# Moving columns of the feed-forward products taken in turn from two places

## The chip, the cores and the metric

The kernel runs on one core of a Trainium2 chip. The metric is the device time of one execution in microseconds. Three executions of the kernel before took 502.5, 500.82 and 500.69 us; their median is 500.82 us. One further execution was profiled. It took 500.46 us, of which 498.7 us lie between its first and its last recorded instruction; that stretch is called the span below, and times inside it are counted from its start.

## The reference, cut to what matters

A gated linear attention over 4 batches, 8 heads, 768 steps and head size 48 gives the rows of a feed-forward part with 384 inputs, 2048 hidden units and 384 outputs.

```python
def _attn_ref(q, k, v, f_logit):
    f = 1.0 / (1.0 + np.exp(-f_logit))
    for t in range(S):
        state = f[:, :, t, :, None] * state + np.einsum('bhd,bhe->bhde', k[:, :, t], v[:, :, t])
        y[:, :, t] = np.einsum('bhd,bhde->bhe', q[:, :, t], state)

def _moe_ref(x, w_in, w_out):
    h = x @ w_in
    relu6 = np.clip(h + 3.0, 0.0, 6.0)
    g = h * relu6 / 6.0
    return (g @ w_out).astype(np.float32)
```

Here x has 3072 rows: 4 batches times 768 steps.

## The kernel before, in words

**Tiling.** The 768 steps are cut into 6 chunks of 128. A unit is one batch and one chunk, so there are 24 units. The attention of a unit ends in rows of x, transposed (features on partitions, steps along the free dimension). The four units of one chunk, one for each batch, make a group with 4 x 128 = 512 columns. The feed-forward part (FF) runs group by group, and in a group over 16 blocks of 128 hidden units, called f.

**Two halves of every number.** A float32 value is held as a high part and a low part, each in the type float32r, which the multiplier array takes in one pass. A product of two values is then three products: high by high, high by low, low by high (the table `P3`). The tile `xts` holds x: for each of 3 blocks of features and each batch 128 high columns and after them 128 low columns, so the high columns of the four batches stand 1 KB apart. The tile `weight` holds both halves of both weight matrices.

**One f of one group.** `mm1` makes 3 x 3 = 9 products of 512 columns into one PSUM bank (L561; the banks are called `pair` and `single`). ScalarE makes the clipped value `tg` out of it (`relu`, L571), VectorE multiplies by h (`gate6`, L575), ScalarE takes the high half `gg` (`ghigh`, L584) and VectorE the low half (`glow`, L588). `mm2` makes 3 x 3 = 9 products from `gg` into three PSUM banks `o`, one for each 128 outputs (L605). In these products the weights stand still in the array, and the 512 columns of `xts` or `gg` move through it; mm1 reads them as four runs of 128, mm2 as one run of 512. After the 16th f the `o` banks are copied to `os` in SBUF, by VectorE (L669) or ScalarE (L671), and sent out by DMA (`put`, L676).

**Exceptions.** The first three f of group 0 are done in two halves of 256 columns (`half_of`, L623 for the first product, L641 for the second). Their second product takes plain float32, with no split: each is one call with 256 columns, and the array is given two instructions for a call (36 matmul instructions for 18 calls). In the last group the third block of outputs is done in two halves of 256 columns (`half_mm2`, L656), and the hidden halves are kept in `xts` in place of `gg`. A slow path for inputs that end a chunk with a very small decay is in the program and does not run with these inputs.

**Order.** All engines follow one list of steps written out by hand (`ORDER`). It fixes the order of every engine's instructions; waits come from what reads and writes what. `warm` steps in the list are products of a constant zero tile in bf16 (L777), whose 512 moving columns are one block of 128 read four times.

The functions that the change touches:

Of the kernel before, what the change touches and what calls it, by code (L numbers as in the profile page):

```python
# [8 lines left out]
F32 = mybir.dt.float32  # L9
# [10 lines left out]
C = 128  # L20
HC = C // 2
# [136 lines left out]
def gla_moe(ctx: ExitStack, tc: tile.TileContext, unit, w, outT):  # L158
# [16 lines left out]
    def bank():  # L175

        n = banks.pop(0) if banks else 0
        return single if n == 4 else pairs[n // 2][:, n % 2]
# [8 lines left out]
    def whole(f, a, cols):  # L187
        return weight[:, f, a * WN:(a + 1) * WN][:, cols]

    def win(f, a, k):  # L190
        return whole(f, a, slice(k * 128, (k + 1) * 128))

    def wout(f, a, m):
        return whole(f, a, slice(DM + m * 128, DM + (m + 1) * 128))
# [356 lines left out]
    def rows_of(g):  # L551
        if "xt" not in g:
            g["xt"] = xts[:, KT:][:, ::-1] if g["odd"] else xts[:, :KT + 1]
        return g["xt"]

    def mm1(g, f):
        h = bank()[:, :g["n"]]
        i = 0
        for a, b in P3:
            for k in range(KT):  # L560
                nc.tensor.matmul(  # L561
                    h, win(f, a, k), g["xt"][:, k, :g["n"] // C, b],
                    start=i == 0, stop=i == 3 * KT - 1,
                )
                i += 1
        g[f] = {"h": h}
# [25 lines left out]
    def outs_of(g, f):  # L592
        if f == 0:
            g["o"] = [
                ps_o.tile([128, 512], F32, tag=f"o{x}", name=f"o{g['name']}_{x}")[:, :g["n"]]
                for x in range(KT)
            ]

    def mm2(g, f, ms=range(KT)):
        if 0 in ms:  # L600
            outs_of(g, f)
        for i in range(3):
            a, b = P3[-i]
            for m in ms:
                nc.tensor.matmul(  # L605
                    g["o"][m], wout(f, a, m), g[f]["gg"][:, b],
                    start=f == 0 and i == 0, stop=f == NF - 1 and i == 2, skip_group_check=True,
                )

    def mm2_whole(g, f):  # L610
        outs_of(g, f)
        for m in range(KT):
            nc.tensor.matmul(
                g["o"][m], wout(f, 1, m).bitcast(F32), g[f]["t"],
                start=f == 0, stop=f == NF - 1, skip_group_check=True,
            )

    def half_of(p):

        def mm1(g, f):  # L620
            h = bank()[:, :256]
            for i, (a, b, k) in enumerate((a, b, k) for a, b in P3 for k in range(KT)):
                nc.tensor.matmul(  # L623
                    h, win(f, a, k), g["xt"][:, k, 2 * p:2 * p + 2, b],
                    start=i == 0, stop=i == 3 * KT - 1,
                )
            g[f, p] = {"h": h}

        def relu(g, f):
            d = g[f, p]  # L630
            d["t"] = sb.tile([128, 512], F32, tag="tg", name=f"th{p}_{f}")[:, :256]
            nc.scalar.activation(d["t"], d["h"], AF.Relu, bias=half, scale=1.0 / 6.0)

        def gate6(g, f):
            d = g[f, p]
            nc.vector.scalar_tensor_tensor(d["t"], d["t"], 1.0, d["h"], op0=ALU.min, op1=ALU.mult)

        def mm2(g, f):
            outs_of(g, f + p)
            for m in range(KT):  # L640
                nc.tensor.matmul(  # L641
                    g["o"][m][:, p * 256:(p + 1) * 256],
                    wout(f, 1, m).bitcast(F32), g[f, p]["t"],
                    start=f + p == 0, stop=False, skip_group_check=True,
                )

        return {"mm1": mm1, "relu": relu, "g": gate6, "mm2": mm2}

    def half_mm2(g, f, part):

        n = g["n"] // 2
        if f == 0:
            g["oh", part] = bank()[:, :n]
        for i in range(3):
            a, b = P3[-i]
            nc.tensor.matmul(  # L656
                g["oh", part], wout(f, a, 2), g[f]["gg"][:, b, part * n:(part + 1) * n],
                start=f == 0 and i == 0, stop=f == NF - 1 and i == 2, skip_group_check=True,
            )

    def out(g, m, part, on_vector):
        n = g["n"] if part is None else g["n"] // 2
        if "os" not in g:
            held = cv.tile([128, 4 * WN + 4], I16, tag="raw", name=f"os{g['name']}")
            g["os"] = held[:, :4 * WN].bitcast(F32).rearrange("p (m n) -> p m n", m=KT)
        os = g["os"][:, m, n * (part or 0):n * (part or 0) + n]
        src = g["o"][m] if part is None else g["oh", part]
        if on_vector:
            nc.vector.tensor_copy(out=os, in_=src)  # L669
        else:  # L670
            nc.scalar.activation(os, src, AF.Copy)  # L671
        g["os", m, part] = os

    def put(g, m, part=None):
        n = (g["n"] if part is None else g["n"] // 2) // C
# [5 lines left out]
    def group(name, n, dst):  # L681
        return {"name": name, "n": n, "dst": dst, "odd": len(groups) % 2}
# [26 lines left out]
    def smallest_flag():  # L709
# [5 lines left out]

    MOE = {
        "mm1": mm1, "relu": relu, "g": gate6, "gh": ghigh, "gl": glow, "mm2": mm2, "mm2x": mm2_whole,
        "mm2m0": lambda g, f: mm2(g, f, [0]), "mm2m1": lambda g, f: mm2(g, f, [1]),
        "mm2p": lambda g, f: half_mm2(g, f, 0), "mm2q": lambda g, f: half_mm2(g, f, 1),
    }  # L720
    for p, part in enumerate("ab"):
        MOE.update({op + part: step for op, step in half_of(p).items()})
    OUT = {
        "outv": lambda g, m: out(g, m, None, True), "outs": lambda g, m: out(g, m, None, False),
        "outh": lambda g, p: out(g, 2, p, p == 0), "od": put, "odh": lambda g, p: put(g, 2, p),
    }
    FLAG = {"flag0": smallest_rows, "flag1": smallest_turn, "flag2": smallest_flag}
# [81 lines left out]
    with tc.If(rv > 0):  # L809
        with tc.For_i(0, B, 1) as b:  # L810
            st = sb.tile([PR, NP, 128], F32, tag="qkf", name="st_s")
            nc.vector.memset(st, 0.0)
            with tc.For_i(0, NCB, 1) as c:
                u = b * NCB + c
                t = sb.tile([PR, 2, NP, C], F32, tag="qkf", name="t_s")
                ft = sb.tile([PR, NP, C], F32, tag="qkf", name="f_s")
                src = qk[bass.ds(u, 1), :PR].rearrange("a p x n c -> p (a x) n c")
                nc.sync.dma_start(out=t, in_=src)
                th = t.rearrange("r x (c n) (o t) -> r x n c o t", c=2, o=2)
                src = fg[bass.ds(u, 1), :PR, 1:].rearrange("a p (n c) -> p (a n) c", n=NP)  # L820
# [3 lines left out]
                for t0 in range(0, C, TS):  # L824
# [29 lines left out]
                g = group("_s", C, lambda m: outT[m * 128:(m + 1) * 128, bass.ds((c * B + b) * C, C)].rearrange(  # L854
                    "m (b t) -> m b t", t=C
                ))
# [3 lines left out]
                for f in range(NF):  # L860
                    for step in (mm1, relu, gate6, ghigh, glow, mm2):
                        step(g, f)
                for m in range(KT):
                    out(g, m, None, m == 1)
                    put(g, m)
# [55 lines left out]
```

## Time and profile before

| quantity | value |
|---|---|
| median of three executions | 500.82 us |
| profiled execution, its own time | 500.46 us |
| span of the profiled execution | 498.7 us |
| TensorE matmul (PE) busy | 485.0 us, 97% |
| TensorE weight load (PEld) busy | 388.7 us, 78% |
| VectorE (DVE) busy | 292.6 us, 59% |
| ScalarE (ACT) busy | 217.6 us, 44% |
| GpSimd (POOL) busy | 53.7 us, 11% |
| mean granted TensorE clock | 0.992 |

In the rows of the profile, `L605 PE MATMUL o<-gg,weight 128*128 128x512 f32 x693 | 173.3, 399` would read: line 605, engine, operation, output tile and input tiles, 128 rows by 128 columns of weights, 128 partitions by 512 moving columns, 693 instructions; then the time during which at least one of them ran, and the mean length of one in ns. Products overlap: the next starts while the last is still on its way through the array. The length of one therefore says little, and the distance from start to start is what a product costs in a row of them.

### The profile page before, as it was taken

The page shows a single profiled execution, that of the slowest core. Times are in us where ns is not written, and L with a number is a line of the kernel's source. Part 1 is how long each engine was busy: PE and PEld are TensorE (multiplying, and loading weights), DVE is VectorE, ACT ScalarE, POOL GpSimd, SP SyncE. Part 2 cuts the span into 40 slices and gives each one's busy share as a digit, 9 for nine tenths or more (in the row PEclk, how much of TensorE's full clock was granted, in tenths as well). Part 3 has the DMA queues.
Part 4 walks back from the last instruction along what each step waited for, and adds up shares of the span by engine and source line. Part 5 has one row for each costly group of instructions (what it writes and reads, how often), then busy time and mean ns, then how long its engine had stood idle before and what let it go on. Part 6 is the DMA issues. An engine that isn't in the chain of part 4 may idle for free.

```text
span 498.7 us, 11481 instructions
## 1 busy us (share of the span) xinstructions
PE 485.0 (97%) x4958; PEld 388.7 (78%) x4958; DVE 292.6 (59%) x462; ACT 217.6 (44%) x372; POOL 53.7 (11%) x57
## 2 busy tenths in 40 slices
PE   8798999999999999999999999999999999999996
PEld 4587787777888888788888888887877888788885
DVE  6969999989684636757405576545642243333341
ACT  5778988754343315433305434224422232333331
POOL 2311521203200110211000010100100000000000
PEclk9979999999999999999999999999999999999999
DMA  8776765442320330523100133300300000100001
GB/s 298 269 256 238 233 207 202 132 140 82 106 83 1 114 97 1 192 75 123 52 0 3 60 130 95 105 8 2 105 24 6 24 2 0 64 0 1 0 1 69
DMA packets 18969, 44.91 MB, mean 90 GB/s; under 512 B 2528, under 2 KB 8544, under 8 KB 18912
## 3 DMA queue, kind: packets, MB, share of 16 engines
q1 hardware_dynamic: 18768, 43.98, 26.7%
q8 instruction: 41, 0.67, 0.6%
q10 hardware_dynamic: 144, 0.13, 0.1%
q14 instruction: 16, 0.13, 0.1%
HBM read 36.43 MB, written 4.72 MB: 83 GB/s over the span
## 4 chain that ended last, share of the span: by engine, by line
PE 86%; DMA 6%; DVE 4%; ACT 2%; issue 0%; POOL 0%; SPq 0%; POOLq 0%; DVEq 0%; ACTq 0%
PE o L605 35%; PE pair L561 25%; PE single L561 12%; DMA raw<-w 3%; PE pair L488 2%; PE pair L505 2%; PE pair L418 2%; PE pair L456 2%; DMA qkf<-unit 1%; PE single L656 1%; PE pair L656 1%; PE o L641 1%; PE pair L437 1%; PE pair L623 1%; DMA v<-unit 1%; DVE w L285 1%
## 5 line engine op out<-in xcount | busy, mean ns | idle before, releaser
L605 PE MATMUL o<-gg,weight 128*128 128x512 f32 x693 | 173.3, 399 | 1.2 <-DVE gg L588 1.2
L605 PEld LDWEIGHTS o<-gg,weight 128*128 128x128 f32 x693 | 128.0, 188 | 32.8 <-DVE gg L588 2.5
L561 PE MATMUL pair<-xts,weight 128*128 128x512 f32 x576 | 142.2, 396 | 0.1
L561 PEld LDWEIGHTS pair<-xts,weight 128*128 128x128 f32 x576 | 107.1, 188 | 24.9 <-DVE weight L293 0.6
L588 DVE TENSOR_TENSOR gg<-tg,gg 128x512 fp32r<-128x512 f32 x77 | 52.6, 687 | 68.4 <-ACT gg L584 68.3
L584 ACT ACTIVATE gg<-tg 128x512 fp32r<-128x512 f32 x77 | 48.2, 629 | 90.9 <-PE o L605 76.2
L575 DVE SCALAR_TENSOR_TENSOR tg<-tg,pair 128x512 f32<-128x512 f32 x64 | 42.8, 682 | 56.4 <-ACT tg L571 56.3
L571 ACT ACTIVATE tg<-pair,half 128x512 f32<-128x512 f32 x64 | 43.4, 685 | 63.0 <-PE pair L561 55.8
L561 PE MATMUL single<-xts,weight 128*128 128x512 f32 x261 | 66.5, 399 | 0.0
L561 PEld LDWEIGHTS single<-xts,weight 128*128 128x128 f32 x261 | 48.2, 188 | 11.0
L374 DVE TENSOR_TENSOR_SCAN gates<-gates,rend 112x516 f32<-112x516 f32 x24 | 33.1, 1380 | 0.2
L571 ACT ACTIVATE tg<-single,half 128x512 f32<-128x512 f32 x29 | 19.8, 683 | 28.0 <-PE single L561 24.9
L350 DVE TENSOR_TENSOR_SCAN suffix<-gates,unit 112x516 f32<-112x516 f32 x24 | 30.4, 1265 | 2.8 <-ACT gates L344 2.8
L363 POOL TENSOR_TENSOR qkf<-qkf,suffix 112x512 f32<-112x512 f32 x13 | 18.8, 1443 | 95.5 <-DVE rend L366 24.1
L379 POOL TENSOR_TENSOR qkf<-qkf,gates 112x512 f32<-112x512 f32 x13 | 17.4, 1345 | 85.1 <-DVE gates L374 40.4
L524 ACT ACTIVATE xts<-pair 112x512 fp32r<-112x512 f32 x24 | 14.3, 596 | 27.2 <-PE pair L456 13.6
L605 PE MATMUL o<-xts,weight 128*128 128x512 f32 x96 | 25.3, 397 | 0.6 <-ACT xts L584 0.6
L575 DVE SCALAR_TENSOR_TENSOR tg<-tg,single 128x512 f32<-128x512 f32 x29 | 19.7, 680 | 10.4 <-ACT tg L571 10.3
L425 DVE TENSOR_TENSOR a<-pair,causal 128x512 f32<-128x512 f32 x24 | 16.4, 682 | 10.6 <-PE pair L505 9.2
L605 PEld LDWEIGHTS o<-xts,weight 128*128 128x128 f32 x96 | 17.8, 188 | 5.4 <-ACT xts L584 1.0
L537 DVE TENSOR_TENSOR xts<-pair,xts 112x512 fp32r<-112x512 f32 x19 | 13.0, 685 | 11.4 <-ACT xts L524 11.4
L588 DVE TENSOR_TENSOR xts<-tg,xts 128x512 fp32r<-128x512 f32 x16 | 11.1, 693 | 11.3 <-ACT xts L584 11.3
(92 smaller groups left out, 449.1 us busy)
## 6 DMA issues: line engine op xcount, KB each, us to landing
qkf<-unit SPq DMA_DIRECT2D x24, 512.0 KB, 4.2
raw<-w SPq DMA_DIRECT2D x16, 768.0 KB, 5.4
gates<-unit SPq DMA_DIRECT2D x24, 258.5 KB, 2.9
v<-unit SPq DMA_DIRECT2D x24, 200.0 KB, 4.1
outT<-os SPq DMA_DIRECT2D x17, 256.0 KB, 2.1
xts<-xts SPq DMA_DIRECT2D x48, 48.0 KB, 2.2
weight<-w SPq DMA_DIRECT2D x3, 192.0 KB, 2.8
outT<-os SPq DMA_DIRECT2D x1, 128.0 KB, 3.7
```

What stands on the lines that cost most here:

```text
L350: nc.vector.tensor_tensor_scan(flat(sf)[:, ::-1], gt[:, 1:][:, ::-1], flat(unit)[:, ::-1], 0.0, op0=ALU.mult, op1=ALU.add,)
L363: engine("kmul", i).tensor_tensor(parts_of(t, 1), parts_of(t, 1), split(sf[:, :, 1:C + 1]), op=ALU.mult)
L374: nc.vector.tensor_tensor_scan(past, past, flat(rend), 0.0, op0=ALU.mult, op1=ALU.add)
L379: engine("qmul", i).tensor_tensor(parts_of(t, 0), parts_of(t, 0), split(to), op=ALU.mult)
L425: nc.vector.tensor_tensor(d["a"].rearrange("r p e t -> r e p t"), d["at"], causal.unsqueeze(1).unsqueeze(1).broadcast_to([128, 2, NP, HC]) ...
L524: nc.scalar.activation(parts(0), d["y"][:PR], AF.Copy)
L561: nc.tensor.matmul(h, win(f, a, k), g["xt"][:, k, :g["n"] // C, b], start=i == 0, stop=i == 3 * KT - 1,)
L571: nc.scalar.activation(d["t"], d["h"], AF.Relu, bias=half, scale=1.0 / 6.0)
L575: nc.vector.scalar_tensor_tensor(d["t"], d["t"], 1.0, d["h"], op0=ALU.min, op1=ALU.mult)
L584: nc.scalar.activation(d["gg"][:, 0], d["t"], AF.Copy)
L588: engine("gl", f if g["name"] == "0" else NU).tensor_tensor(d["gg"][:, 1], d["t"], d["gg"][:, 0].bitcast(F32), op=ALU.subtract)
L605: nc.tensor.matmul(g["o"][m], wout(f, a, m), g[f]["gg"][:, b], start=f == 0 and i == 0, stop=f == NF - 1 and i == 2, skip_group_check=True,)
```

## The change

Every moving operand of an FF product is read in another order. In `mm1`, instead of batch 0, then batch 1, then 2, then 3, a column of batch 0 is followed by the same step's column of batch 1, and so on for 128 steps; then the same with batches 2 and 3. In `mm2`, in each 256 columns a column of the first 128 is followed by one of the second 128. The stored tiles keep their layout; only the access patterns of the products change. Since the product writes its output columns in the order in which they come in, `h`, `tg` and `gg` now have mixed columns, and the `o` banks have them mixed twice: column 4c + q of each 256 belongs to place 64q + c. The copies to `os` undo this: they read PSUM in order and write to SBUF with a step of 64 columns (256 bytes) from one element to the next. Of the products that run, L561, L605, L623, L641 and L656 change (L614, in `mm2_whole`, is in no step of the list). The attention, the conversion of the weights, the sizes and counts of all instructions, and the order of instructions on every engine are as before (line numbers apart).

```diff
+    def turned(x):
+        if x.shape[1] == 1:
+            return x
+        return x.rearrange("p (h b) c -> p h c b", b=2)
+
+    def halves_of(x):
+        if x.shape[1] % 256:
+            return x
+        return x.rearrange("p (h b c) -> p h c b", b=2, c=128)
+
     def mm1(g, f):
...
-                    h, win(f, a, k), g["xt"][:, k, :g["n"] // C, b],
+                    h, win(f, a, k), turned(g["xt"][:, k, :g["n"] // C, b]),
...
     def mm2(g, f, ms=range(KT)):
...
-                    g["o"][m], wout(f, a, m), g[f]["gg"][:, b],
+                    g["o"][m], wout(f, a, m), halves_of(g[f]["gg"][:, b]),
...
     def mm2_whole(g, f):
...
-                g["o"][m], wout(f, 1, m).bitcast(F32), g[f]["t"],
+                g["o"][m], wout(f, 1, m).bitcast(F32), halves_of(g[f]["t"]),
...
     def half_of(p):
...
-                    h, win(f, a, k), g["xt"][:, k, 2 * p:2 * p + 2, b],
+                    h, win(f, a, k), turned(g["xt"][:, k, 2 * p:2 * p + 2, b]),
...
-                    wout(f, 1, m).bitcast(F32), g[f, p]["t"],
+                    wout(f, 1, m).bitcast(F32), halves_of(g[f, p]["t"]),
...
     def half_mm2(g, f, part):
...
-                g["oh", part], wout(f, a, 2), g[f]["gg"][:, b, part * n:(part + 1) * n],
+                g["oh", part], wout(f, a, 2), halves_of(g[f]["gg"][:, b, part * n:(part + 1) * n]),
...
     def out(g, m, part, on_vector):
...
         src = g["o"][m] if part is None else g["oh", part]
+        g["os", m, part] = os
+        if n % 256 == 0:
+            os = os.rearrange("p (h q c) -> p h c q", q=4, c=HC)
+            src = src.rearrange("p (h c q) -> p h c q", q=4, c=HC)
         if on_vector:
             nc.vector.tensor_copy(out=os, in_=src)
         else:
             nc.scalar.activation(os, src, AF.Copy)
-        g["os", m, part] = os
```

## The prediction, made before the changed kernel ran

> **What bounds the kernel now.** I read the page first: busy shares, the chain of waits, the costliest groups.
>
> ```profile
> span 498.7 us, 11481 instructions
> PE 485.0 (97%) x4958; PEld 388.7 (78%) x4958; DVE 292.6 (59%) x462; ACT 217.6 (44%) x372; POOL 53.7 (11%) x57
> PE 86%; DMA 6%; DVE 4%; ACT 2%; issue 0%; POOL 0%; SPq 0%; POOLq 0%; DVEq 0%; ACTq 0%
> L605 PE MATMUL o<-gg,weight 128*128 128x512 f32 x693 | 173.3, 399 | 1.2 <-DVE gg L588 1.2
> L561 PE MATMUL pair<-xts,weight 128*128 128x512 f32 x576 | 142.2, 396 | 0.1
> L561 PE MATMUL single<-xts,weight 128*128 128x512 f32 x261 | 66.5, 399 | 0.0
> ```
>
> TensorE is busy nearly all the time and makes up 86% of the chain that ended last, and the products that the change touches (L605, L561) are by far the largest groups in it. So what one of these products costs in a row of them sets the time. The view by stretches (time; PE, PEld, DVE, ACT, POOL busy; clock) says where this holds:
>
> ```profile
> 60.00:110.00 50.00, 48.66 (x508) 38.16 (x507) 47.66 (x75) 37.98 (x56) 10.50 (x7) 1.00 0.54 178
> 110.00:200.00 90.00, 90.00 (x1057) 72.79 (x1056) 59.58 (x94) 34.00 (x65) 11.56 (x10) 1.00 0.21 68
> 200.00:300.00 100.00, 100.00 (x1034) 80.93 (x1033) 54.89 (x87) 35.80 (x64) 10.82 (x10) 1.00 0.25 79
> 300.00:420.00 120.00, 119.82 (x1114) 96.49 (x1113) 55.47 (x87) 40.12 (x72) 5.06 (x5) 1.00 0.12 39
> 434.00:487.00 53.00, 53.00 (x263) 44.40 (x262) 18.48 (x30) 17.88 (x27) 0.00 (x0) 1.00 0.00 1
> ```
>
> From 110 us on TensorE alone is full, at full granted clock; VectorE is at two thirds or less. Before 110 us VectorE is full too (47.66 of 50 us), so a quicker product buys little there.
>
> **What a product costs.** The next rows are pieces of the chain (start, length, what, count), then one of the view by stretches for the bf16 products of L777 alone.
>
> ```profile
> 173.02 10.49 PE pair L561 x45
> 183.52 8.40 PE o L605 x36
> 491.72 1.07 PE single L656 x9
> 46.10 1.31 PE o L641 x6
> 7.72:8.80 1.08, 1.08 (x5) 0.49 (x6) 1.00 1.01 384
> ```
>
> mm1: 10.49 / 45 = 233.1 ns for 512 columns. mm2: 8.40 / 36 = 233.3 ns. The half of L656: 1.07 / 9 = 119 ns for 256 columns. A bf16 product of 512 columns took 1.08 / 5 = 216 ns, at the same clock of 1.00. Plain float32 (L641) took 1.31 / 6 = 218 ns for an instruction of 256 columns; if each column passes twice, as the length suggests, that is 218 ns for 512 passes. So the array can take a column in 0.42 ns, and float32r products lose 17 ns in 512 columns and about 10 in 256: a loss mostly by column. It is gone where a column has half the bytes (bf16) or twice the time (plain float32), so it lies in bringing in 4 bytes for every column, not in the array or the PSUM write. Where mm1 jumps 1 KB between its four runs, it costs the same as mm2's single run, so a jump now and then is free.
>
> **The change part by part.**
>
> *Reading in turn.* Two streams now give every other column. The trace has no product that jumps at every column, so I bound it. Below: each place gets twice the time for its next word, as in L641, and the whole loss goes: 233.2 − 216 = 17 ns less. Above: a read brings two neighbouring words, of which one is now used, so a product takes twice as long: 233 ns more. Between them stands ScalarE, which reads every second word in L251:
>
> ```profile
> L251 ACT ACTIVATE w<-raw 128x768 int32<-128x768 uint32 x16 | 14.5, 904 | 0.2 <-DVE weight L293 0.2
> L290 ACT ACTIVATE weight<-w 128x768 fp32r<-128x768 f32 x16 | 13.4, 840 | 5.0 <-DVE w L285 5.0
> ```
>
> It pays 904 − 840 = 64 ns for 768 words, 0.083 ns a word; at that price a product would cost 43 ns more. I take the lower end, −17 ns. [...] That is a choice, not a proof, and both other ends stay as rivals.
>
> Now the count. The view by stretches of each line alone gives the products after 110 us:
>
> ```profile
> 110.00:420.00 310.00, 139.90 (x571) 105.95 (x569) 1.00 0.19 60
> 420.00:434.00 14.00, 5.93 (x25) 4.69 (x26) 1.00 0.16 57
> 434.00:498.70 64.70, 30.15 (x121) 21.64 (x119) 0.99 0.04 14
> 110.00:420.00 310.00, 146.55 (x590) 109.45 (x591) 1.00 0.19 60
> 420.00:434.00 14.00, 7.59 (x29) 4.92 (x27) 1.00 0.16 57
> 434.00:498.70 64.70, 23.22 (x90) 16.85 (x90) 0.99 0.04 14
> ```
>
> L561 (first three rows) and L605: 571 + 25 + 121 + 590 + 29 + 90 = 1426 products. 1426 x 17 ns = 24.2 us. L656 adds 96 halves at 10 ns: 1.0 us. Before 110 us there are 1626 − 1426 = 200 more (693 + 96 + 576 + 261 in all); 200 x 17 = 3.4 us, but VectorE is full there, so I count 0.5 us. Plain float32 (L641) shows no loss and gains nothing. Together −25.7 us.
>
> *Copies that restore the order.* Eighteen in full or half (L669, L671) now write with 256 bytes between elements. Unchanged in number, reads in order. Most lie under mm1 of the next group, which writes other banks. Where they lie on the chain:
>
> ```profile
> 427.02 1.08 ACT os L671 x2
> 428.10 0.58 ACT tg L571
> 429.44 0.64 ACT xts L584
> 430.12 1.22 PE o L605 x3
> 493.89 0.38 ACT os L671
> L285 DVE SCALAR_TENSOR_TENSOR w<-top,w 128x768 int16<-128x768 int16 x16 | 16.8, 1049 | 0.5
> L575 DVE SCALAR_TENSOR_TENSOR tg<-tg,pair 128x512 f32<-128x512 f32 x64 | 42.8, 682 | 56.4 <-ACT tg L571 56.3
> L636 DVE SCALAR_TENSOR_TENSOR th<-th,pair 128x256 f32<-128x256 f32 x5 | 2.0, 418 | 1.0 <-ACT th L632 1.0
> ```
>
> At 427 us two copies on ScalarE precede the first `relu` of the last group, and TensorE waits behind them; at 494 us the last half copy ends the kernel. The nearest spaced write is L285 (2 bytes in every 4): 768 elements in 1049 ns, where the step from L636 to L575 (264 ns for 256) makes 682 + 264 = 946 for an even write: 0.13 ns an element, 70 ns a copy. Free at the one end, twice as long at the other (0.54 us each at 427, 0.38 at the end: +1.5 us). I take 0.1 us each, +0.3 us.
>
> *The wait that gets longer.* At 430 us TensorE stands idle for the chain of ScalarE and VectorE from those copies. Its own mm1 ahead of it gets 9 x 17 ns = 0.15 us shorter, so the idle time grows by that: +0.2 us. In the rest of the last group an f takes 2.10 us of mm1 and 0.70 of mm2, and the steps between them 0.69 + 0.69 + 0.63 + 0.69 = 2.7 us; mm2 runs one mm1 later than its own, so over 1 us of slack is left when an f shrinks from 2.8 to 2.6 us.
>
> **The sum.** 498.7 − 25.7 + 0.3 + 0.2 = 473.5 us of span. The profiled run had 500.46 − 498.7 = 1.8 us outside the span, and the median is 0.4 us above that run: 475.7. I forecast **476 us**, 5% faster. Half the loss removed would give 488; the full loss without any give-back 473 or a little less. The forecast's own range is 470 to 498.
>
> **The rivals.**
>
> *A. The order of reading does not matter.* If the loss is a ceiling on bytes that come in (512 columns of 4 bytes in 233 ns), two streams share it as one did. For it: mm1 and mm2, with different runs, cost 233.1 and 233.3 ns. Against it: it needs a ceiling that sits just 7% under what the array takes. Time: 500.8 + 0.3 for the copies = 501 us.
>
> *B. Every jump costs a read.* If words come in pairs and the second is thrown away, a product takes 466 ns: 1426 x 233 = 332 us, 96 x 119 ns = 11 us, and the early products, 200 x 233 + 54 x 119 ns = 53 us, nearly all to be paid, since TensorE is almost full there too (48.66 of 50): about 890 us. At ScalarE's price of 43 ns it would be 1426 x 43 ns = 61 us: about 565. For it: L251 pays something. The loss itself says that reading has no slack: two words at a time at just the pace needed would show no loss in bf16 and plain float32, and a small one here. Against it: 17 ns is far from a doubling, and where each column comes from one of only two places, a pair once read can serve twice if it is kept.
>
> [...]
>
> *C. Reading gains nothing and the spaced copies hurt.* At 427 us both copies stand ahead of a `relu` that TensorE waits for, and a group's `o` banks are freed only by its copies. It decides from about +0.9 us a copy on (2 at 427, 1 at the end, 2.7 us). At 1 us more each, and as much at the four other group ends where mm1 no longer covers them: 503.5 to 508 us.
>
> **Chances.** Forecast (loss wholly or partly gone) 0.54; A 0.21; B 0.18; C or another small loss 0.07. Measurement can tell about 0.5%, that is 2.5 us, from no change. So faster 0.54, same 0.21, slower 0.25. The range 470 to 512 holds nearly all of the forecast, A and C, together 0.8, and leaves out B, which would lie far above.
>
> **What would show it.** Right: nine products of mm1 in the chain fall from 2.10 us to about 1.95, mm2 likewise, nine halves of L656 from 1.07 to about 0.98, L641 stays at 1.31 for six, and TensorE stays full after 110 us. Pieces of 2.10 us as before mean A; of 4 us, or 2.5, mean B. Longer L669 and L671 with longer idle time before L605 at the group ends mean C. The forecast is also wrong if the products get quicker but VectorE or ScalarE chains fill the gap: then TensorE's busy share falls while the span stays.

## The result and the profile after

The changed kernel took 480.86 us (median of four executions, 476.12 to 481.75) against 500.75 us for the kernel before, measured beside it: a ratio of 0.958 with a 95% interval of 0.951 to 0.965. It is faster, as forecast, by 4.2% where 5% was forecast. Ratios are those of fast executions: one of e10_both (533.4 us, granted clock 0.844) and one of e12_second_only (493.61 us, 0.986), both below, are slow ones and stay out of them. The profiled execution took 481.13 us with a span of 479.4 us. In the changed kernel L561 has become L573, L605 L617, L641 L653, L656 L668, and the copies L669 and L671 have become L685 and L687.

The same pieces of the chain of waits as in the prediction (start, length, what, count), now of the changed kernel:

```profile
172.28 9.71 PE pair L573 x45
181.99 7.77 PE o L617 x36
471.09 1.00 PE single L668 x9
46.38 1.64 PE o L653 x6
409.93 1.98 ACT os L687 x2
411.91 0.45 ACT tg L583
413.79 0.70 PE o L617 x2
473.13 0.60 ACT os L687
```

A product of 512 columns now costs 9.71 / 45 = 215.8 ns in the first matrix and 7.77 / 36 = 215.8 ns in the second: what the bf16 product took (216 ns), with nothing left of the 17 ns. The half of L668 fell from 119 to 111 ns. Against that, plain float32 (L653) rose from 218 to 273 ns an instruction, and the copies are far slower than assumed: two on ScalarE take 1.98 us instead of 1.08, the half copy at the end 0.60 instead of 0.38.

The page's groups say the same of all copies and of the idle time before the second product (`| idle before`), which was 1.2 and 0.6 us:

```profile
L617 PE MATMUL o<-gg,weight 128*128 128x512 f32 x693 | 161.4, 383 | 2.5 <-DVE gg L600 2.4
L617 PE MATMUL o<-xts,weight 128*128 128x512 f32 x96 | 23.7, 381 | 1.6 <-ACT xts L596 1.5
L653 PE MATMUL o<-th,weight 128*128 128x256 f32 x36 | 10.8, 435 | 0.0
L687 ACT ACTIVATE os<-o 128x512 f32<-128x512 f32 x11 | 11.4, 1090 | 8.2 <-PE o L617 8.2
L685 DVE COPY os<-o 128x512 f32<-128x512 f32 x6 | 6.4, 1064 | 8.6 <-PE o L617 8.6
```

And the view by stretches (time; PE, PEld, DVE, ACT, POOL busy; granted clock), with five rows of the changed kernel and then the first product alone, up to 110 us, in the kernel before and in the changed one:

```profile
0.00:60.00 60.00, 53.27 (x793) 38.92 (x794) 46.43 (x76) 43.90 (x75) 13.69 (x25) 0.89 0.76 259
60.00:110.00 50.00, 46.74 (x598) 38.33 (x597) 47.95 (x75) 41.81 (x58) 10.50 (x6) 1.00 0.53 182
110.00:200.00 90.00, 89.65 (x1168) 77.50 (x1167) 65.04 (x104) 36.70 (x70) 13.57 (x12) 1.00 0.23 73
200.00:300.00 100.00, 100.00 (x1097) 87.14 (x1097) 59.23 (x92) 41.53 (x72) 10.21 (x10) 1.00 0.26 85
300.00:420.00 120.00, 118.15 (x1023) 102.09 (x1022) 56.59 (x88) 42.29 (x72) 5.10 (x5) 1.00 0.11 36
...
0.00:110.00 110.00, 30.78 (x124) 23.02 (x125) 0.97 0.67 224
...
0.00:110.00 110.00, 26.62 (x113) 20.85 (x114) 0.94 0.66 224
```

In the first 60 us this execution was granted 0.89 of the clock. By 110 us it had begun 113 of the first products, the kernel before 124 (the second products stand at 81 in both): the changed kernel was 11 products, some 2.4 us, behind there, and made its gain afterwards, with TensorE nearly full again.

### The profile page after: what moved, and what is told of

The parts are those of the page before. It is cut to its first block, busy times and chain, and to the rows that moved or that the text cites. A ratio compares the mean times of both kernels' runs of the same rounds, so it can differ in the third digit from the quotient of the medians.

```text
span 479.4 us, 11485 instructions
## 1 busy us (share of the span) xinstructions
PE 460.9 (96%) x4958; PEld 391.5 (82%) x4958; DVE 295.9 (62%) x462; ACT 225.4 (47%) x372; POOL 53.1 (11%) x57
## 4 chain that ended last, share of the span: by engine, by line
PE 80%; DVE 8%; DMA 4%; ACT 4%; issue 2%; SPq 0%; POOL 0%; DVEq 0%; ACTq 0%
PE o L617 32%; PE pair L573 22%; PE single L573 10%; DMA raw<-w 3%; PE pair L488 2%; PE pair L505 2%; PE o L653 2%; PE pair L418 2%; PE pair L456 2%; PE pair L635 1%; PE pair L668 1%; PE single L668 1%; DMA v<-unit 1%; DVE w L285 1%; DVE tg L587 1%
## 5 line engine op out<-in xcount | busy, mean ns | idle before, releaser
L617 PE MATMUL o<-gg,weight 128*128 128x512 f32 x693 | 161.4, 383 | 2.5 <-DVE gg L600 2.4
L617 PEld LDWEIGHTS o<-gg,weight 128*128 128x128 f32 x693 | 128.8, 189 | 22.2 <-DVE gg L600 4.1
L573 PE MATMUL pair<-xts,weight 128*128 128x512 f32 x576 | 132.7, 381 | 0.8 <-DVE weight L293 0.8
L573 PEld LDWEIGHTS pair<-xts,weight 128*128 128x128 f32 x576 | 107.5, 189 | 16.3 <-DVE weight L293 1.2
L600 DVE TENSOR_TENSOR gg<-tg,gg 128x512 fp32r<-128x512 f32 x77 | 53.8, 703 | 58.2 <-ACT gg L596 57.9
L573 PE MATMUL single<-xts,weight 128*128 128x512 f32 x261 | 62.2, 383 | 0.0
L573 PEld LDWEIGHTS single<-xts,weight 128*128 128x128 f32 x261 | 48.4, 189 | 6.7
L617 PE MATMUL o<-xts,weight 128*128 128x512 f32 x96 | 23.7, 381 | 1.6 <-ACT xts L596 1.5
L617 PEld LDWEIGHTS o<-xts,weight 128*128 128x128 f32 x96 | 17.9, 189 | 4.7 <-ACT xts L596 1.9
L456 PE MATMUL pair<-v,ktok 64*48 64x48 f32 (+1 forms) x768 | 15.0, 213 | 4.7 <-issue 2.7
```

Source lines behind the costliest of these rows:

```text
L456: nc.tensor.matmul(d["kv"][r:r + m, odd, c, n], d["ktok"][rs, 2 * n + part, r:r + m], heads_of(vt[rs], part, n, e)[:, :D], start=(odd, e) ...
L573: nc.tensor.matmul(h, win(f, a, k), turned(g["xt"][:, k, :g["n"] // C, b]), start=i == 0, stop=i == 3 * KT - 1,)
L600: engine("gl", f if g["name"] == "0" else NU).tensor_tensor(d["gg"][:, 1], d["t"], d["gg"][:, 0].bitcast(F32), op=ALU.subtract)
L617: nc.tensor.matmul(g["o"][m], wout(f, a, m), halves_of(g[f]["gg"][:, b]), start=f == 0 and i == 0, stop=f == NF - 1 and i == 2, skip_group ...
```

## The experiments

Three theories went in. **S**: a stream of 4-byte words cannot give one per column without rest; two streams have twice the time each. **N**: the loss comes from taking neighbouring words one right after the other; any other step removes it. **P**: a read brings neighbours, every jump costs a read, and two places only get away with it because a pair once read is kept. (P is rival B's mechanism, with the pair kept.)

In all of these kernels "first product" is mm1, "second product" mm2.

### One place with a step, two places, four places

Four kernels read the first product in one mixed order and the second in the order that undoes it, so the copies stay as they were before the change.

```diff
# e1_undo
     mm1:  x.rearrange("p (h b) c -> p h c b", b=2)
     mm2:  x.rearrange("p (h c b) -> p h b c", b=2, c=128)
# e2_step2 (r=2), e3_step4 (r=4)
     mm1:  x.rearrange("p j (c r) -> p j r c", r=r)
     mm2:  x.rearrange("p (j r c) -> p j c r", r=r, c=128 // r)
# e4_four, groups 1 to 4 (groups 0 and 5 as e1_undo)
     mm1:  x.rearrange("p j c -> p c j")
     mm2:  x.rearrange("p (c j) -> p j c", j=4)
```

Expected of e1_undo: 

> The first product reads as in the change (two batches in turn, 1 KB apart). The second reads each run of 256 mixed columns with a step of 2 words from one place, first the even then the odd ones, which puts the order right, so the copies write in order as before the change. Theory S (the loss goes because two streams deliver in turn, each with twice the time): first product 216 ns from start to start, second 233 ns or more, copies 0.59 and 0.69 us, about 488 us in all. Theory N (the loss comes from taking neighbouring words one right after the other; any step of 2 words or more removes it, one place or two): both 216 ns, about 477 us, 2 to 4 us under the change. Theory P (a jump alone costs a read, and two places only hide it because a read pair is kept): second product well over 233 ns.

Expected of e2_step2: 

> The first product reads every batch's 128 columns with a step of 2 words from one place (even columns, then odd); the second takes two places 256 bytes apart in turn, which puts the order right; copies in order. S: first product 233 ns or more, second 216. N: both 216, about 477 us. P: first product well over 233 ns, second 216.

Expected of e3_step4: 

> The first product reads each batch's 128 columns with a step of 4 words (16 bytes) from one place; the second takes four places 128 bytes apart in turn; copies in order. S: first product 233 ns or more, second 216 ns. N: both 216 ns. [...]

Expected of e4_four: 

> In groups 1 to 4 the first product takes the four batches in turn (four places 1 KB apart) and the second reads with a step of 4 words from one place; groups 0 and 5 as in the run with a step of 2 words in the second product; copies in order. S: four places are as good as two (216 ns), the second product 233 ns or more. N: both 216 ns. P: four places cost more than two, the step of 4 words costs more than the step of 2.

Measured, as ratios to the kernel before (499.3 us beside them): e1_undo 1.336 [1.331, 1.342], e2_step2 1.362 [1.357, 1.367], e3_step4 1.467 [1.461, 1.473], e4_four 1.416 [1.411, 1.420]. The longest pieces of the chain, for e1_undo, e2_step2, e3_step4 and e4_four in turn, the first product above the second (L567 and L611 in the first three, L574 and L618 in e4_four):

```profile
208.38 9.71 PE pair L567 x45
218.10 16.33 PE o L611 x36
...
230.72 20.40 PE pair L567 x45
251.12 7.77 PE o L611 x36
...
240.06 20.80 PE pair L567 x45
260.86 9.72 PE o L611 x36
...
214.55 12.30 PE pair L574 x45
226.85 16.56 PE o L618 x36
```

A step of 2 words in one place costs 16.33 / 36 = 454 or 20.40 / 45 = 453 ns, a step of 4 words 462 or 460 ns: nearly the doubling that rival B priced at 466. Two places give 216 ns at 1 KB and at 256 bytes. Four places give 12.30 / 45 = 273 ns at 1 KB and 9.72 / 36 = 270 ns at 128 bytes. N falls at once: a step in one place does not remove the loss, it nearly doubles the price. S had four places as good as two and falls there. P, by which a jump costs a read, had the signs right: a step in one place costs, four places cost more than two, and the step of 4 words costs more than the step of 2. The two steps differ by only 6 to 9 ns; within one place nearly all of the price comes with leaving the direct neighbour (233 ns in order).

### Runs of words, and what the copies cost

```diff
# e5_runs, second product of groups 1, 2, 3, 4 with r = 2, 4, 8, 16
+        return x.rearrange("p (b c r) -> p c b r", b=2, r=2 ** int(g["name"]))
```

> The changed kernel, where the second product of groups 1, 2, 3 and 4 takes runs of 2, 4, 8 and 16 words in turn from two places 1 KB apart (groups 0 and 5 as in the change). The restoring of the order in the copies is left out, so the columns go out mixed. Theory K (a read brings a pair of neighbouring words and one pair per place is kept; the loss of one stream comes where pair follows pair from one place): runs of 2 words cost 216 ns, and the loss comes back as the runs get longer, to about 225 ns with 4 and 230 ns with 8 and 16. Theory S (each stream needs a rest after every word): already runs of 2 words cost 225 ns or more, runs of 16 words 233. Theory L (the loss belongs to longer pieces, 64 bytes or so, at whose end one stream stalls): runs of 2, 4 and 8 words all cost 216 ns, runs of 16 words 233.

The chain's pieces of the second product in groups 1, 2, 3 and 4 of e5_runs (one execution, 504.04 us):

```profile
187.68 12.10 PE o L622 x36
...
266.88 13.32 PE o L622 x54
...
346.72 8.77 PE o L622 x36
...
394.17 8.64 PE o L622 x36
```

Runs of 2 words cost 12.10 / 36 = 336 ns, of 4 words 13.32 / 54 = 247, of 8 words 244, of 16 words 240. All are above the 233 ns of one place read in order, and runs of 2 are the worst. This fits none of the three theories it was priced for. That a pair from one place followed by a pair from the other should be bad (336 ns), while single words in turn cost 216 ns, speaks against "pairs are read and kept" as I had it.

Three runs take the restoring of the order and the plain float32 products by themselves. Each was timed in five rounds beside the kernel before (498.8 us).

```diff
# e6_mixed_out: copies in order; on the host
-    outs = r.results[0]["outT"].reshape(DM, NCB, B, C)
-    return np.ascontiguousarray(outs.transpose(2, 1, 3, 0)).reshape(NT, DM)
+    outs = r.results[0]["outT"].reshape(DM, NCB, 2, HC, 2, 2)
+    return np.ascontiguousarray(outs.transpose(2, 4, 1, 5, 3, 0)).reshape(NT, DM)
# e7_read_spaced: PSUM is read with a step of 4 words, SBUF written in order
-            os = os.rearrange("p (h q c) -> p h c q", q=4, c=HC)
-            src = src.rearrange("p (h c q) -> p h c q", q=4, c=HC)
+            os = os.rearrange("p (h q c) -> p h q c", q=4, c=HC)
+            src = src.rearrange("p (h c q) -> p h q c", q=4, c=HC)
# e8_pairs_plain: only in the halved hidden blocks of group 0
     mm1:  x.rearrange("p b (h c) -> p b c h", h=2)
     mm2:  t.rearrange("p (b c h) -> p c b h", b=2, h=2)
```

> The changed kernel, with copies that write in order; the columns leave the chip mixed, and the transposition on the host that was there already takes them in the other order. Measures the restoring by itself. If its cost is the 0.5 us of each copy in ScalarE, twice at the last group's start and the half copy at the end, the time falls by 1.2 to 2 us (0.2% to 0.4%) under the change; if restoring costs nothing on the path, it is the same; if copies hold up the group ends too, 3 us or more.

> The changed kernel, with copies that read PSUM with a step of 4 words and write SBUF in order. If the extra 0.37 to 0.49 us of a copy comes from the spaced write, copies go back to 0.59 and 0.69 us and the time is that of the mixed output (about 479 us); if spaced access costs the same on either side, copies stay at 1.06 to 1.08 us and the time that of the change (481).

> The changed kernel, where the plain float32 products of the three halved hidden blocks read pairs of words in turn from two places instead of single words (their first product takes two places 256 bytes apart, so the columns end in the same order). K (pairs kept or used up at once): an instruction of 256 columns costs 216 to 227 ns instead of 271, 36 x 50 ns = 1.8 us less on TensorE before 60 us, of which VectorE hides part: 0 to 2 us less in all. S: it stays near 271 ns.

Ratios to the kernel before: e6_mixed_out 0.953 [0.950, 0.957], e7_read_spaced 0.956 [0.953, 0.958], e8_pairs_plain 0.958 [0.955, 0.960]. The change itself stands at 0.958 in both of its measurements, so the times alone show little; the rows show the terms. The copies of e7_read_spaced and the plain float32 products of e8_pairs_plain:

```profile
L687 ACT ACTIVATE os<-o 128x512 f32<-128x512 f32 x11 | 6.2, 591 | 8.2 <-PE o L617 8.2
L685 DVE COPY os<-o 128x512 f32<-128x512 f32 x6 | 4.1, 686 | 8.6 <-PE o L617 8.6
...
L654 PE MATMUL o<-th,weight 128*128 128x256 f32 x36 | 9.2, 389 | 0.0
```

Reading PSUM with a step of 4 words costs these copies nothing (591 and 686 ns; 590 and 689 before the change); the whole extra cost sat in the spaced write to SBUF: 1090 − 590 = 500 ns on ScalarE, 1064 − 689 = 375 ns on VectorE. Plain float32 took 8.8 us in order, 10.8 us with single words in turn, 9.2 us with pairs in turn (busy time of the 36 instructions; from start to start 216, 271 and 227 ns each). The 227 ns are what K priced, but K fails for float32r in e5_runs. So in these plain float32 products runs of 2 words are better than single words (227 against 271 ns), the opposite of float32r (336 against 216 ns).

### How near the two places may be, and the sum by halves

```diff
# e9_places, second product of groups 1 to 4
+        if g["name"] == "1":
+            return x.rearrange("p (n b c) -> p n c b", b=2, c=4)
+        if g["name"] == "2":
+            return x.rearrange("p (n b c) -> p n c b", b=2, c=16)
+        if g["name"] == "3":
+            return x[:, :256].unsqueeze(2).broadcast_to([128, 256, 2])
+        if g["name"] == "4":
+            return gg.rearrange("p b n -> p (b n)")[:, 510 * b + 1:510 * b + 513]
```

> The changed kernel with other reads of the second product: group 1 takes two places 16 bytes apart in turn (four words from each, then the next 32 bytes), group 2 two places 64 bytes apart, group 3 reads every one of 256 columns twice in a row, group 4 reads 512 columns in order from one place that starts on an odd word. In group 2 the first product reads in order, as before the change. Left out: the restoring of the order in the copies, and in groups 3 and 4 the right columns. If what matters is that consecutive columns come from two places, however near: 216 ns in groups 1 and 2. If they must lie in different banks that change with some higher address bit: 330 ns or more in group 1, as with a step of 4 words in one place (460 ns). If the loss of one stream comes from the number of new bytes per column: reading each column twice costs 216 ns. If pairs start on 8 bytes: the odd start costs 300 ns or more; if not, 233 ns. First product of group 2: 233 ns.

Pieces of the chain of e9_places (one execution, 482.75 us): second product of group 1, of group 2, the first product of group 2 in order, then the second of group 3 and of group 4:

```profile
155.23 1.94 PE o L630 x9
...
229.54 1.94 PE o L630 x9
...
242.44 8.36 PE pair L585 x36
...
289.90 1.94 PE o L630 x9
...
373.19 8.44 PE o L630 x36
```

Two places 16 bytes apart cost 1.94 / 9 = 216 ns, 64 bytes apart 216 ns: of the distances tried, from 16 bytes to 1 KB, none matters. Every column taken twice in a row costs 216 ns. In the same execution the first product read in order costs 232 ns, so the loss belongs to the order and not to this kernel. An odd start in one place costs 8.44 / 36 = 234 ns, about what the even one does, so a pair that starts on 8 bytes is not what a stream needs.

Last, the change once more, its best version, and half of it, timed on one chip beside the kernel before (499.7 us).

```diff
# e10_both: e7_read_spaced and e8_pairs_plain together
# e11_change: no edit
# e12_second_only: the first products in order, the copies restore an order of two
-                    h, win(f, a, k), turned(g["xt"][:, k, :g["n"] // C, b]),
+                    h, win(f, a, k), g["xt"][:, k, :g["n"] // C, b],
```

> The change with spaced reads of PSUM in the copies (writes in order) and pairs of words for the plain float32 products. Copies 0.59 and 0.69 us, plain float32 227 ns. If the two gains add: 1 to 3 us under the change on the same chip, the best version; if the early part hides the second: that of the spaced reads alone.

> The change once more, as the measure for the other runs on this chip. If the low granted clock early in the profiled run was chance: about 478 us where the kernel before takes 498.8, with granted clocks of 0.98 to 0.998. If the change brings it about: granted clocks under 0.99 in nearly every run, 480 us or more.

> Only the second products read in turn from two places, the first ones in order; the copies restore an order of two. The sum by terms: first product 233 ns, second 216 ns; 709 of the 1426 products after 110 us gain 17 ns, 12.1 us, and the copies and the longer wait give back 2.5 us: about 10 us under the kernel before, 489 us where that takes 498.8. If the gain of the one hangs on the other (both needed), 497 us or more.

Ratios: e10_both 0.953 [0.948, 0.958], e11_change 0.958 [0.954, 0.962], e12_second_only 0.983 [0.978, 0.987]. The two products of e12_second_only, and the copies at the start of the last group in e10_both and in e11_change:

```profile
167.42 10.46 PE pair L573 x45
177.87 7.77 PE o L617 x36
...
407.91 1.09 ACT os L689 x2
...
408.46 1.98 ACT os L687 x2
```

e12_second_only has 232 ns in the first product and 216 in the second, and comes to 0.983 x 499.7 = 491 us, where 489 was expected (by the interval 6 to 11 us are saved; about 10 were expected). The rows show that the gain of the one product does not hang on the other. e10_both is 0.9 us quicker at the copies and has the lowest ratio of the versions that give the same order on the chip; its interval overlaps that of the change, so 2 us better is what the rows make likely, not what the times prove.

## Why the prediction was right, point by point

**What a product gains.** Taken as −17 ns for 512 columns and −10 for 256; measured 233.2 − 215.8 = 17.4 and 119 − 111 = 8. The choice of the lower end was right. After 110 us TensorE stayed nearly full, as the prediction needed: 89.65 of 90 us, 100 of 100, and 118.15 of 120 with the start of the last group in it. Added up from start to start over the whole trace, the FF products after 110 us took 25.2 us less, which is what the sum had for them.

What the choice of the lower end rested on fared worse; it was the author's estimate, as no row of the kernel before shows a product that jumps at every column. "A jump now and then is free" held for mm1's four runs (233.1 against 233.3 ns) and does not carry over to a jump at every column: a step of 2 words in one place costs 454 ns. "Each place gets twice the time for its next word" would make four places at least as good as two, and they cost 270 to 273 ns. Plain float32 (L641), the prediction's example of a stream with time to spare, lost by the same reading in turn. So the size of the gain was well bounded from the rows, but that two places reach it, and four do not, is more than the argument could give. In that part the prediction was lucky.

**Plain float32.** "Shows no loss and gains nothing": the size of this term was wrong. It lost 273 − 218 = 55 ns an instruction, 36 x 55 ns = 2.0 us, all before 60 us.

**The copies.** Taken at 0.1 us each, from a row where 2 bytes in 4 are written; they cost 0.50 (ScalarE) and 0.38 us (VectorE), close to the end of the range that the prediction had kept ("twice as long"). The row chosen steps 4 bytes from element to element, the copy 256; no run tries the steps between, so that this makes the difference is likely and not shown. In e12_second_only the copies write in turn to two places 512 bytes apart, and took 1115 ns (ScalarE) and 1087 ns (VectorE): for these writes two places in turn are no cheaper. On the path: 0.90 us at the last group's start, 0.22 us at the end, and a later issue of an output behind it (see the sum). The idle time before the second products grew by 1.3 us in the groups with `gg`, nearly all of it before 110 us (2.4 us there against 1.2), where VectorE is full (47.95 of 50 us from 60 to 110 us), and by 1.0 us in the last one, where +0.2 was forecast beside the copies; most of that 1.0 us is the copies' 0.90 seen from TensorE. In e10_both, whose copies write in order, it is 0.8 us against the 0.6 of the kernel before, the +0.2 that was forecast.

**The early part.** Forecast 0.5 us ahead at 110 us, found about 2.4 us behind. Plain float32 costs 2.0 us there, of which the quicker first products give back about 1. What is left goes with the clock: 0.89 in the first 60 us, 0.94 in the profile of the kernel before. That is not the change's doing as far as the runs tell. In e11_change, without any edit, the clock in this stretch was 0.94, as in the kernel before, and by 110 us it had begun 120 of the first products and 81 of the second: 4 products, some 0.9 us, behind. In e12_second_only the clock was 1.00. The rows of the two:

```profile
0.00:60.00 60.00, 52.63 (x812) 37.87 (x816) 46.60 (x77) 45.28 (x77) 14.28 (x25) 0.94 0.77 261
...
0.00:60.00 60.00, 55.76 (x909) 40.38 (x910) 52.49 (x86) 47.95 (x82) 16.09 (x26) 1.00 0.80 276
```

The ten executions of the change ran from 476.1 to 481.8 us with granted clocks of 0.981 to 0.998, those of the kernel before from 496.8 to 502.8 us with 0.988 to 0.999 where they were recorded. Whether the change lowers the chance of an early full clock a little stays open.

**The sum.** The span fell by 498.7 − 479.4 = 19.3 us, against 25.2 forecast. Matched instruction by instruction, in order of start, the 1401st of the 4958 matmul instructions starts at 110.2 us in the kernel before and at 112.5 in the changed one, the last at 493.6 and 472.8. That splits the missing 5.9 us in three.

- Before 110 us, 2.8 us: 2.3 behind instead of 0.5 ahead. The longer idle time before the second products of the `gg` groups lies here.
- From there to the last product, 1.7 us: 23.1 gained where 24.8 were forecast. The FF products gave their 25.2. The wait at the last group's start grew by 0.9 instead of the 0.4 of copies and wait. About 1.1 us are new waits among the products of the attention, which the prediction did not have.
- After the last product, 1.4 us: 1.5 us longer, where 0.1 was forecast. The half copy is 0.22 us of it. Behind it, SyncE took 2.0 us to issue one output, at 472.8 us, where it takes 0.3 us for the others.

The last stands in the rows of the output issues (shortest, median, longest in ns) of the kernel before, the changed kernel and e10_both:

```profile
L676 SPq DMA_DIRECT2D outT<-os x18: 332/343/440, 121.9 to 493.3; - x18
...
L691 SPq DMA_DIRECT2D outT<-os x18: 332/344/2033, 125.0 to 472.8; - x18
...
L693 SPq DMA_DIRECT2D outT<-os x18: 332/344/440, 123.0 to 469.8; - x18
```

The four runs whose copies write spaced (the changed kernel, e8_pairs_plain, e11_change, e12_second_only) have a longest issue of 1.3 to 2.0 us, the three whose copies write in order (e6_mixed_out, e7_read_spaced, e10_both) 0.44. Behind the end of the last copy the four have 5.1 to 5.7 us of span left, e7_read_spaced and e10_both 4.4 to 4.5. So it goes with the spaced write; why is not shown.

**The rivals.** A (order does not matter) is out: 216 against 233 ns in one execution. B's price was real, 454 ns against 466, but its condition was not met: it decides when one place is read with a step, not when two are read in turn. A step of 2 words in one place cost 453 ns, hardly less than a step of 4 (462), and two places in turn 216. C's point of +0.9 us a copy was not reached: the copies lost 0.38 to 0.50 us.

**Why two places help.** The runs give the rule but not the mechanism. S is backed by the columns taken twice (216 ns) and by two places, and has four places (270 to 273 ns) and runs of two (336 ns) against it. P is backed by the steps and by four places, and has runs of two and the odd start against it. What the read path fetches and keeps stays open.

## What to carry to other kernels

Where TensorE is full, measure the distance from start to start of each kind of product and compare the kinds: a class that costs more per column than another on the same array (here 233 ns against 216 for 512 columns) may have its loss in what feeds it, and then the order of the moving columns is worth a try. For the float32r products here, read in order, two places taken word by word in turn were worth 7% of each product (233 to 216 ns), and any other order of separate columns tried cost more, up to nearly double (462 ns). Put a mixed order right where a spaced access was free in these copies (reading PSUM, 591 ns on ScalarE) rather than where it was dear (writing SBUF, 1090 ns), and look at every data type that the same edit touches: what helped float32r hurt plain float32 (218 to 273 ns an instruction).

## What the runs showed that was not expected

One table holds what a product of 512 float32r columns costs from start to start, by the order of its reads: each column twice 216 ns; two places word by word 216 (16, 64, 256, 512 bytes and 1 KB apart); one place in order 232 to 234; runs of 16, 8, 4 and 2 words from two places 240, 244, 247 and 336; four places 270 to 273; one place with a step of 2 words 453, of 4 words 460 to 462. Plain float32 orders them otherwise: its 36 instructions took 8.8 us in order, 9.2 with pairs in turn, 10.8 with single words in turn from places 512 bytes apart and 12.5 from places 256 bytes apart (e2_step2); 9.2 also with a step of 2 words in one place (e1_undo), where float32r takes nearly double, and 16.8 from four places in turn (e3_step4). And a copy that writes 4-byte elements 256 bytes apart takes 1.06 to 1.09 us for 512, on either engine, while one that reads PSUM with a step of 16 bytes takes what an even one takes (591 and 686 ns against 590 and 689).
